# Two MLPs behind a sigmoid attention: transposes ahead of the copies, weight splits off GpSimd, output products opened early

## The chip, the cores and the metric

The kernel runs on one core of one Trainium2 chip. The time is the device time of one execution in microseconds, as the median of a few runs. The profile is of one execution; its engines are called PE (TensorE, with PEld for its weight loads), DVE (VectorE), ACT (ScalarE), POOL (GpSimd) and SP (which issues most DMAs).

## The reference

All tensors arrive as 32-bit floats, the weights of the MLPs as 64-bit floats.

```python
def attn(q, k, v):                      # 4 batches, 12 heads, 448 positions, 64 per head
    scores = 1 / sqrt(64) * q @ k.T - log(448)
    return 1 / (1 + exp(-scores)) @ v
def reference(q, k, v, ...):
    x = attn(q, k, v)                   # as 1792 tokens x 768
    h = x @ w_in1                       # 768 -> 2048
    x = (h - tanh(h)) @ w_out1          # 2048 -> 768
    h = x @ w_in2
    return (s * relu(h) ** 2 + b) @ w_out2
```

## The kernel before

The tokens are cut into two halves of 896 (two batches each). For each half the kernel runs attention for 12 pairs of heads, then layer 1, then layer 2. The instructions of each engine keep the order of the program text (`InOrder`), so the order in which the code is written is the order in which an engine takes its work, and an instruction that waits holds up all behind it on its engine.

**Attention.** `prep(i)` transposes q and k of pair i on PE into one PSUM tile of two banks (`tqk`), four transposes for q and four for k; ACT copies the q half to `qt`, DVE the k half to `kt`. `qk` makes the scores (`sc`) and the sigmoid (`af`, ACT), `av` the product with v (`o`), which ACT and DVE split into a high and a low part (`x`). Pair i+1 is prepared between the two halves of pair i's scores.

**Precision.** A product of two 32-bit values is made of three matmuls (`mm3`): high x high, high x low and low x high. The high part is a rounding copy by ACT, the low part a subtraction on DVE or POOL.

**Weights.** They come in chunks of 128 x 768. A group is four `in` chunks (f = 0 to 3), then two `out` chunks for each half `hd` of the output; there are four groups in a layer and eight group passes in a half of the tokens. Three steps run ahead of use: `w_load` (five chunks ahead), `w_conv` (three ahead, only in the first half of the tokens: ACT `wy` and three DVE instructions that write `wa`, `wa` and `wf` make a 32-bit float out of a 64-bit one, which is also kept in DRAM for the second half), and `w_split` (two ahead: ACT writes `whi`, DVE or POOL `wlo`). POOL has the `wlo` of the `out` chunks in the first half of the tokens. `w_ahead(n)` runs these steps; it is called from `hidden` (part "a" after the first block of tokens, part "b" after the second, as `fill` between the instructions of `activate`; for f = 3 only after all) and after some output products.

**Layers.** `hidden` makes one f: 18 matmuls on 512 tokens, 18 on 384 (`h`), and `activate` turns each block into `g`. In layer 1 an output product `y` is one d of three in a half: two PSUM banks, four f, two blocks of three matmuls. In layer 2 an output product `z` is one tile of 128 tokens, twelve matmuls of 384 columns. `bank` hands out five PSUM banks in turn for `h`, `y` and `z`. The outcome is copied by ACT in group 0 and added by DVE in the others; in the last group of layer 1 it is also split into `x2`, the input of layer 2.

Of the kernel before, what the change touches and what calls it, by code (L numbers as in the profile page):

```python
# [9 lines left out]
F32 = mybir.dt.float32  # L10
# [3 lines left out]
ALU = mybir.AluOpType  # L14
# [5 lines left out]
def tile_kernel(ctx, tc, q, k, v, w_in1, w_out1, w_in2, w_out2, s_in, b_in, out):  # L20
# [140 lines left out]

    done = {w_load: 0, w_conv: 0, w_split: 0}
# [60 lines left out]
    def prep(i):  # L223

        if i >= B * NP:
            return
        b = i // NP
        rq, rk, rr = (raws[i][nm] for nm in "qkr")
        both = banks("tqk")

        def transposed(ps, r, first):
# [12 lines left out]
        ready[i] = qt, kt  # L244
        avs[i] = []

# [47 lines left out]

    pos = [0]

    def hidden(layer, x, last, order=None):

        p = pos[0]
        pos[0] += 1  # L300
        w = w_t.pop(p)
        gt = g_p.tile([P, 2, T2], F32R, tag="g", name="g", bufs=4)
        ps, left = {}, [CC, CC]
        for step in order or ((0, range(CC)), (1, range(CC))):
            if callable(step):
                step()
                continue
            i, ccs = step
            n = BLOCKS[i].stop - BLOCKS[i].start
# [12 lines left out]

# [6 lines left out]
    def layer1(sb, order):  # L329

        x = [x_t[sb, cc] for cc in range(CC)]
        y_t, x2 = {}, []
        for grp in range(FC // FG):
            g = [hidden(0, x, f == FG - 1, order if grp == 0 and f == 0 else None) for f in range(FG)]
            for hd in range(2):
                ws = out_pair()
                for d in range(3):
                    dm = hd * 3 + d
                    ps = [bank("y")[:, :ns.stop - ns.start] for ns in BLOCKS]
                    for f in range(FG):  # L340
                        for i, ns in enumerate(BLOCKS):
                            o = f % 2 * HM + d * P
                            mm3(ps[i], ws[f // 2], slice(o, o + P), g[f], ns, f == 0, f == FG - 1)
                    if grp == 0:
                        y_t[dm] = x_p.tile([P, T2], F32, tag="y", name="y", bufs=7)
                    y = y_t[dm]
                    if grp == FC // FG - 1:
                        x2.append(x_p.tile([P, 2, T2], F32R, tag="x", name="x2", bufs=CC))
                    for i, ns in enumerate(BLOCKS):
                        if grp == 0:  # L350
                            act.copy(y[:, ns], ps[i])
                            continue
                        dve.tensor_tensor(out=y[:, ns], in0=ps[i], in1=y[:, ns], op=ALU.add)
                        if grp == FC // FG - 1:
                            split(x2[dm][:, 0, ns], x2[dm][:, 1, ns], y[:, ns])
                    if d < 2:
                        now(w_ahead(pos[0] - 2 + d))
        return x2

    def store(sb, t, z, cs):  # L360
# [9 lines left out]
    def layer2(sb, x, beside):  # L370

        z_t = {}
        for grp in range(FC // FG):
            g = [hidden(1, x, f == FG - 1) for f in range(FG)]
            for hd in range(2):
                cs = slice(hd * HM, (hd + 1) * HM)
                ws = out_pair()
                for t in range(T2 // P):
# [4 lines left out]
                    ps = bank("z")[:, :HM]  # L383
                    ts = slice(t * P, t * P + P)
                    for f in range(FG):
                        wh, wl = ws[f // 2]
                        fs = slice(f % 2 * HM, f % 2 * HM + HM)
                        pe.matmul(ps, g[f][:, 0, ts], wh[:, fs], start=f == 0, stop=False)
                        pe.matmul(ps, g[f][:, 0, ts], wl[:, fs], start=False, stop=False)
                        pe.matmul(ps, g[f][:, 1, ts], wh[:, fs], start=False, stop=f == FG - 1)  # L390
                    z = z_t[t]
                    if grp == 0:
                        act.copy(z[:, cs], ps)
                    else:
                        dve.tensor_tensor(out=z[:, cs], in0=ps, in1=z[:, cs], op=ALU.add)
# [20 lines left out]
    for sb in range(B // 2):  # L416
# [20 lines left out]
        layer2(sb, x2, {} if last else {2: lambda: prep(i1), 4: lambda: qk(i1, 0), 6: lambda: qk(i1, 1)})  # L437


# [28 lines left out]
```

## Time and profile before

| | |
|---|---|
| median of 3 runs | 1220.09 us (1220.08 to 1222.82) |
| the profiled execution: its own time, its span | 1218.4 us, 1216.6 us |
| PE busy | 1139.4 us, 94% of the span |
| PEld, DVE, ACT, POOL busy | 948.7, 561.2, 489.4, 67.4 us |
| mean granted PE clock | 0.986 of full |
| DMA | 123.62 MB, 102 GB/s |

The span runs from the first to the last instruction; the execution's own time is 1.8 us more. PE is the engine that is nearly always busy, and what is to be looked for is the 77 us in which it is not, and who ends each of these gaps. A PE row gives the start of a merged run of matmuls and, in brackets, how long PE sat idle before it and on whose work. Matmuls overlap, so a row's duration is longer than its step to the next row.

### The profile page before, as it was taken

How to read it: one execution, taken by the hardware profiler on the slowest of the kernel's cores; microseconds unless marked ns; L12 is line 12 of the kernel's file. 1: busy time of each engine (PE TensorE's matmuls, PEld its weight loads, DVE VectorE, ACT ScalarE, POOL GpSimd, SP SyncE). 2: the span in 40 equal slices, each digit the busy share in tenths (PEclk: the TensorE clock that was granted, in tenths of full speed). 3: DMA queues.
4: the chain of work that ended last, by engine and by line, in shares of the span. 5: the costliest groups of instructions: out<-in, count | busy, mean ns of one | idle time of the engine just before them, and what ended most of it. 6: DMA issues, size and time to landing. Idle time of an engine off the chain costs nothing. (4 is left out here: it accounts for less than half of the span.)

```text
span 1216.6 us, 14407 instructions
## 1 busy us (share of the span) xinstructions
PE 1139.4 (94%) x5760; PEld 948.7 (78%) x5760; DVE 561.2 (46%) x773; ACT 489.4 (40%) x734; POOL 67.4 (6%) x62
## 2 busy tenths in 40 slices
PE   7999999999989898989899999999999999999998
PEld 3445888888868897979784448888888889898988
DVE  0232757676676566665721114143434641434343
ACT  4664444242436453443525553330403352606060
POOL 0000102010110101020200000000000000000000
PEclk9999999999999898989899999999999999999999
DMA  5553454545444435444344311212121111111102
GB/s 145 138 161 92 156 174 144 166 141 167 144 137 136 155 117 156 144 135 150 105 139 104 85 34 39 65 39 65 40 66 49 55 53 53 52 53 45 60 13 91
DMA packets 111970, 123.62 MB, mean 102 GB/s; under 512 B 53024, under 2 KB 87328, under 8 KB 111904
## 3 DMA queue, kind: packets, MB, share of 16 engines
q1 hardware_dynamic: 110016, 122.25, 33.3%
q8 instruction: 45, 0.74, 0.2%
q10 hardware_dynamic: 1888, 0.46, 0.2%
q14 instruction: 21, 0.17, 0.0%
HBM read 92.01 MB, written 30.67 MB: 101 GB/s over the span
## 5 line engine op out<-in xcount | busy, mean ns | idle before, releaser
L79 PE MATMUL h<-x,whi 128*128 128x512 f32 (+1 forms) x1536 | 435.7, 364 | 4.3 <-ACT x L79 4.3
L79 PEld LDWEIGHTS h<-x,whi 128*128 128x128 f32 x1536 | 284.2, 188 | 40.1 <-ACT x L79 4.7
L79 PE MATMUL h<-x,wlo 128*128 128x512 f32 (+1 forms) x768 | 280.2, 365 | 0.0
L79 PE MATMUL z<-whi,g 128*128 128x384 f32 x896 | 238.1, 344 | 25.4 <-ACT whi L79 25.4
L79 PE MATMUL y<-g,whi 128*128 128x512 f32 (+1 forms) x768 | 219.3, 367 | 3.8 <-ACT whi L79 3.5
L79 PEld LDWEIGHTS z<-whi,g 128*128 128x128 f32 x896 | 167.7, 194 | 29.3 <-ACT whi L79 28.0
L79 ACT ACTIVATE t<-h 128x512 f32<-128x512 f32 (+1 forms) x128 | 69.7, 544 | 252.1 <-PE h L79 251.8
L79 PE MATMUL z<-wlo,g 128*128 128x384 f32 x448 | 154.4, 345 | 8.8 <-POOL wlo L79 6.5
L79 PEld LDWEIGHTS y<-g,whi 128*128 128x128 f32 x768 | 142.0, 188 | 23.1 <-ACT whi L79 6.3
L79 ACT CAST whi<-wf 128x768 fp32r<-128x768 f32 x128 | 105.3, 830 | 128.0 <-DVE wf L79 54.3
L79 PEld LDWEIGHTS h<-x,wlo 128*128 128x128 f32 x768 | 144.5, 188 | 15.2
L79 PE MATMUL y<-g,wlo 128*128 128x512 f32 (+1 forms) x384 | 141.7, 369 | 8.5 <-POOL wlo L79 7.5
L79 DVE TENSOR_TENSOR g<-t,g 128x512 fp32r<-128x512 f32 (+1 forms) x128 | 82.1, 641 | 88.8 <-ACT g L79 88.8
L79 DVE TENSOR_TENSOR wlo<-wf,whi 128x768 fp32r<-128x768 f32 x96 | 91.6, 954 | 56.1 <-ACT whi L79 56.1
L79 ACT ACTIVATE af<-sc,nlogs 128x896 f32<-128x896 f32 x96 | 89.1, 1007 | 55.2 <-PE sc L79 44.0
L79 PEld LDWEIGHTS z<-wlo,g 128*128 128x128 f32 x448 | 87.0, 194 | 11.2 <-POOL wlo L79 8.0
L79 DVE SCALAR_TENSOR_TENSOR wf<-wy,wa 128x768 uint32<-128x768 uint32 x64 | 89.0, 1391 | 3.8
L79 DVE TENSOR_TENSOR z<-z 128x384 f32<-128x384 f32 x84 | 46.4, 557 | 92.6 <-PE z L79 92.5
L79 PEld LDWEIGHTS y<-g,wlo 128*128 128x128 f32 x384 | 72.1, 188 | 20.6 <-POOL wlo L79 9.7
L79 POOL TENSOR_TENSOR wlo<-wf,whi 128x768 fp32r<-128x768 f32 x32 | 62.0, 1938 | 442.7 <-ACT whi L79 243.3
L79 ACT CAST g<-t 128x512 fp32r<-128x512 f32 (+1 forms) x128 | 72.6, 567 | 33.5 <-DVE t L79 31.2
L79 DVE TENSOR_TENSOR t<-h,t 128x512 f32<-128x512 f32 x64 | 39.9, 623 | 93.2 <-ACT t L79 93.2
(34 smaller groups left out, 692.2 us busy)
## 6 DMA issues: line engine op xcount, KB each, us to landing
raw<-in_moe_w_in_dram SPq DMA_DIRECT2D x32, 768.0 KB, 4.9
raw<-in_moe_w_out_dram SPq DMA_DIRECT2D x32, 768.0 KB, 4.7
win<-wf SPq DMA_DIRECT2D x32, 384.0 KB, 2.6
wout<-wf SPq DMA_DIRECT2D x32, 384.0 KB, 2.7
wf<-win SPq DMA_DIRECT2D x32, 384.0 KB, 2.9
wf<-wout SPq DMA_DIRECT2D x32, 384.0 KB, 3.1
rawq<-in_q_dram SPq DMA_DIRECT2D x48, 96.0 KB, 2.7
rawv<-in_v_dram SPq DMA_DIRECT2D x24, 192.0 KB, 2.6
```

Source lines behind the costliest of these rows:

```text
L79: return lambda *a, **kw: tc.keep_in_program_order(getattr(self.engine, name)(*a, **kw))
```

## The change

Four edits. In `prep` all eight transposes come ahead of the two copies. In `w_split` the low part is always made by DVE. In `hidden` the second `out` chunk is split right after the activation of f = 2, and layer 2's first f takes five sixths of both blocks before the last sixth. In both layers the output products of the first half `hd = 0` are opened with f = 0 to 2 (two of them in layer 1, three in layer 2) before their f = 3 matmuls come.

```diff
@@ w_split
         act.copy(hi, t)
         yield
-        eng = pool if 4 <= n < len(a_pass) and chunks[n][0] == "out" else dve
-        eng.tensor_tensor(out=lo, in0=t, in1=hi.bitcast(F32), op=ALU.subtract)
+        dve.tensor_tensor(out=lo, in0=t, in1=hi.bitcast(F32), op=ALU.subtract)
@@ prep
-        act.copy(qt, transposed(both[:, 0], rq, b % 2))
-        dve.tensor_copy(kt, transposed(both[:, 1], rk, 1 - b % 2))
+        tq, tk = transpose(both[:, 0], rq, b % 2), transpose(both[:, 1], rk, 1 - b % 2)
+        act.copy(qt, tq)
+        dve.tensor_copy(kt, tk)
@@ hidden
-                fill = iter(()) if last else w_ahead(p, "a" if left[1 - i] else "b")
+                fill = iter(()) if f == FG - 1 else w_ahead(p, "a" if left[1 - i] else "b")
                 activate(layer, ps[i], gt[:, 0, BLOCKS[i]], gt[:, 1, BLOCKS[i]], fill)
-        if last:
+                if f == FG - 2 and not left[1 - i]:
+                    now(upto(w_split, p + 3))
+        if f == FG - 1:
             now(w_ahead(p))
@@ layer1
+                def products(ds, fs):
+                    for d in ds:
+                        for i, ns in enumerate(BLOCKS):
+                            if fs[0] == 0:
+                                ps[d, i] = bank("y")[:, :ns.stop - ns.start]
+                        for f in fs:
+                            for i, ns in enumerate(BLOCKS):
+                                o = f % 2 * HM + d * P
+                                mm3(ps[d, i], ws[f // 2], slice(o, o + P), g[f], ns, f == 0, f == FG - 1)
...
+                if hd == 0:
+                    products((0, 1), range(FG - 1))
+                    products((0,), [FG - 1])
+                else:
+                    products((0,), range(FG))
+                evict(0)
+                now(w_ahead(pos[0] - 2))
+                if hd == 0:
+                    products((1,), [FG - 1])
+                else:
+                    products((1,), range(FG))
+                evict(1)
+                now(w_ahead(pos[0] - 1))
+                products((2,), range(FG))
+                evict(2)
@@ layer2
-            g = [hidden(1, x, f == FG - 1) for f in range(FG)]
+            g = [hidden(1, x, f, order if grp == 0 and f == 0 else None) for f in range(FG)]
...
+                if hd == 0:
+                    for t in range(3):
+                        products(t, range(FG - 1))
                 for t in range(T2 // P):
...
+                    products(t, [FG - 1] if hd == 0 and t < 3 else range(FG))
...
-                    if t in (0, 3):
+                    if t in (1, 3):
                         now(w_ahead(pos[0] - 2 + t // 3))
@@ the caller of layer2
+        order = [(0, range(CC - 1)), (1, range(CC - 1)), (0, [CC - 1]), (1, [CC - 1])]
+        layer2(sb, x2, order, {} if last else {2: lambda: prep(i1), 4: lambda: qk(i1, 0), 6: lambda: qk(i1, 1)})
```

`evict(d)` holds the copy, add and split that stood behind a product before.

PE in attention, the transposes of the third pair of heads, before (a bracket is what the instruction waits for):

```order
L79 MATMUL tqk<-ident,rawr 128x128 [waits DMAHW3_49,DMAHW0_49,PE_49]
L79 MATMUL tqk<-ident,rawq 128x128 [waits DMAHW7_49,DMAHW6_49]
L79 MATMUL tqk<-ident,rawq 128x128 x2
L79 MATMUL tqk<-ident,rawr 128x128 [waits Activation_49]
L79 MATMUL tqk<-ident,rawk 128x128 [waits DMAHW2_49,DMAHW1_49]
L79 MATMUL tqk<-ident,rawk 128x128 x2
L79 MATMUL sc<-qt,kt 128x448 [waits PE_49]
```

The same place of the changed kernel:

```order
L79 MATMUL tqk<-ident,rawr 128x128 [waits DMAHW3_49,DMAHW0_49,PE_49]
L79 MATMUL tqk<-ident,rawq 128x128 [waits DMAHW7_49,DMAHW6_49]
L79 MATMUL tqk<-ident,rawq 128x128 x2
L79 MATMUL tqk<-ident,rawr 128x128
L79 MATMUL tqk<-ident,rawk 128x128 [waits DMAHW2_49,DMAHW1_49]
L79 MATMUL tqk<-ident,rawk 128x128 x2
L79 MATMUL sc<-qt,kt 128x448 [waits Activation_49]
```

The order of PE's rows is the same; the first transpose for k no longer waits for ACT, and the scores behind it carry the wait for an earlier ACT instruction.

ACT at the end of the first group's f = 2 and through f = 3 in layer 1, before (`t_1059` and `t_1084` are the two blocks of f = 3):

```order
L79 CAST whi<-wf 128x768
L79 CAST g<-t_1030 128x384
L79 ACTIVATE t_1059<-h 128x512
L79 CAST g<-t_1060 128x512
L79 ACTIVATE t_1084<-h 128x384
L79 CAST g<-t_1085 128x384
L79 ACTIVATE wy<-raw 128x768
L79 CAST whi<-wf 128x768
```

The same place of the changed kernel (`t_1063` and `t_1088` are the blocks of f = 3):

```order
L79 CAST whi<-wf 128x768
L79 CAST g<-t_1030 128x384
L79 CAST whi<-wf 128x768
L79 ACTIVATE t_1063<-h 128x512
L79 CAST g<-t_1064 128x512
L79 ACTIVATE t_1088<-h 128x384
L79 CAST g<-t_1089 128x384
L79 ACTIVATE wy<-raw 128x768
```

The high part of the second `out` chunk has moved from behind f = 3's activation and a conversion to ahead of both; the DVE's low part moves with it.

PE at the start of the first output products of that group, from f = 2 of the first product on, before (`g_973` is f = 2, `g_1039` f = 3; `y_1105` and `y_1106` are the banks of the first product, `y_1149` the first bank of the second):

```order
L79 MATMUL y_1105<-g_973,whi_1101 128x512 x2
L79 MATMUL y_1105<-g_973,wlo_1102 128x512
L79 MATMUL y_1106<-g_973,whi_1101 128x384 x2
L79 MATMUL y_1106<-g_973,wlo_1102 128x384
L79 MATMUL y_1105<-g_1039,whi_1101 128x512 x2
L79 MATMUL y_1105<-g_1039,wlo_1102 128x512
L79 MATMUL y_1106<-g_1039,whi_1101 128x384 x2
L79 MATMUL y_1106<-g_1039,wlo_1102 128x384
L79 MATMUL y_1149<-g_830,whi_1033 128x512 x2
```

The same place of the changed kernel (`y_1125` and `y_1126` are now the second product):

```order
L79 MATMUL y_1105<-g_973,whi_1039 128x512 x2
L79 MATMUL y_1105<-g_973,wlo_1040 128x512
L79 MATMUL y_1106<-g_973,whi_1039 128x384 x2
L79 MATMUL y_1106<-g_973,wlo_1040 128x384
L79 MATMUL y_1125<-g_830,whi_1033 128x512 x2
L79 MATMUL y_1125<-g_830,wlo_1034 128x512
L79 MATMUL y_1126<-g_830,whi_1033 128x384 x2
L79 MATMUL y_1126<-g_830,wlo_1034 128x384
```

Eighteen matmuls of the second product now stand between f = 2 and f = 3 of the first.

## Rows read from the trace of the kernel before

**Rows 1.** Groups of PE instructions: count, busy us, mean ns, idle before and releasers.

```profile
L79 PE MATMUL z<-whi,g 128*128 128x384 f32 x896 | 238.1, 344 | 25.4 <-ACT whi L79 25.4
L79 PE MATMUL y<-g,whi 128*128 128x512 f32 (+1 forms) x768 | 219.3, 367 | 3.8 <-ACT whi L79 3.5
L79 PE MATMUL z<-wlo,g 128*128 128x384 f32 x448 | 154.4, 345 | 8.8 <-POOL wlo L79 6.5 <-DVE wlo L79 2.2
L79 PE MATMUL y<-g,wlo 128*128 128x512 f32 (+1 forms) x384 | 141.7, 369 | 8.5 <-POOL wlo L79 7.5 <-DVE wlo L79 1.0
L79 PE MATMUL tqk<-ident,rawr 128*128 128x128 f32 x48 | 16.0, 332 | 22.2 <-ACT qt L79 15.9 <-DMA rawr<-in_q_dram 5.5 <-DMA rawq<-in_q_dram 0.7
```

**Rows 2.** Timeline of one pair in attention: start us, us, instruction, idle before it.

```profile
46.14 0.33 PE L79 MATMUL tqk<-ident,rawr 128*128 128x128 f32 x1
...
47.48 0.33 PE L79 MATMUL tqk<-ident,rawr 128*128 128x128 f32 x1 [0.68 <-ACT qt L79]
...
48.06 3.28 PE L79 MATMUL sc<-qt,kt 64*128 64x448 f32 x16
48.23 0.62 DVE L79 COPY kt<-tqk 128x448 f32<-128x448 f32 x1 [0.78 <-PE tqk L79]
...
49.19 3.70 ACT L79 ACTIVATE af<-sc,nlogs 128x896 f32<-128x896 f32 x4 [1.77 <-PE sc L79]
```

**Rows 3.** PE timeline, layer 1, first half, groups 1 and 2.

```profile
203.21 0.73 PE L79 MATMUL y<-g,whi 128*128 128x512 f32 x2 [0.87 <-ACT whi L79]
...
264.56 0.73 PE L79 MATMUL y<-g,whi 128*128 128x512 f32 x2 [0.87 <-ACT whi L79]
```

**Rows 4.** Chain that ended last, second half of the tokens: start us, us, what.

```profile
881.38 26.72 PE y L79 x130
908.11 29.08 PE h L79 x144
...
940.68 26.72 PE y L79 x130
...
1000.65 28.20 PE z L79 x161
...
1062.11 28.19 PE z L79 x161
```

**Rows 5.** PE timeline, layer 2, first half, groups 0 and 3.

```profile
397.18 0.69 PE L79 MATMUL z<-whi,g 128*128 128x384 f32 x1 [4.21 <-ACT whi L79]
...
598.11 0.69 PE L79 MATMUL z<-whi,g 128*128 128x384 f32 x1 [4.20 <-ACT whi L79]
```

**Rows 6.** PE's matmuls of z in one stretch: busy, PEclk, DMA share, GB/s.

```profile
399.40:404.00 4.60, 4.56 (x14) 0.50 0.60 173
```

**Rows 7.** All engines, layer 1's third group: PE, PEld, DVE, ACT, POOL, PEclk, DMA.

```profile
290.00:350.00 60.00, 56.22 (x275) 49.34 (x274) 41.84 (x54) 21.88 (x35) 8.24 (x4) 1.00 0.46 147
```

**Rows 8.** Timelines of POOL and DVE in and after that group.

```profile
326.00 2.12 POOL L79 TENSOR_TENSOR wlo<-wf,whi 128x768 fp32r<-128x768 f32 x1 [7.43 <-ACT whi L79]
...
326.49 2.44 DVE L79 SCALAR_TENSOR_TENSOR wf<-wy,wa 128x768 uint32<-128x768 uint32 x1
...
354.07 0.96 DVE L79 SCALAR_TENSOR_TENSOR wf<-wy,wa 128x768 uint32<-128x768 uint32 x1
```

**Rows 9.** Timeline where layer 2 begins in the first half.

```profile
362.85 0.68 DVE L79 TENSOR_TENSOR y<-y 128x512 f32<-128x512 f32 x1
...
364.24 1.52 PE L79 MATMUL h<-x,whi 128*128 128x512 f32 x2 [4.26 <-ACT x L79]
...
365.96 0.56 DVE L79 TENSOR_TENSOR x<-y,x 128x384 fp32r<-128x384 f32 x1 [0.58 <-ACT x L79]
...
369.96 0.39 PE L79 MATMUL h<-x,whi 128*128 128x512 f32 x1
```

**Rows 10.** Groups of DVE and POOL: the low parts of the weights.

```profile
L79 DVE TENSOR_TENSOR wlo<-wf,whi 128x768 fp32r<-128x768 f32 x96 | 91.6, 954 | 56.1 <-ACT whi L79 56.1
L79 POOL TENSOR_TENSOR wlo<-wf,whi 128x768 fp32r<-128x768 f32 x32 | 62.0, 1938 | 442.7 <-ACT whi L79 243.3 <-DVE wa L79 170.2 <-issue 20.2
```

More of the change, by code (lines that the diff above doesn't have):

```diff
@@ L229, in prep, with transpose @@
         both = banks("tqk")
-        def transposed(ps, r, first):
+        def transpose(ps, r, first):
             o = 0 if first else SM
@@ L295, in tile_kernel, with hidden @@
     pos = [0]
-    def hidden(layer, x, last, order=None):
+    def hidden(layer, x, f, order=None):
         p = pos[0]
@@ L333, in layer1, with evict @@
         for grp in range(FC // FG):
-            g = [hidden(0, x, f == FG - 1, order if grp == 0 and f == 0 else None) for f in range(FG)]
+            g = [hidden(0, x, f, order if grp == 0 and f == 0 else None) for f in range(FG)]
             for hd in range(2):
                 ws = out_pair()
-                for d in range(3):
-                    dm = hd * 3 + d
[L339 to L343, printed above, removed]
+                ps = {}
+                def products(ds, fs):
[7 more added lines that the diff above has]
+                                mm3(ps[d, i], ws[f // 2], slice(o, o + P), g[f], ns, f == 0, f == FG - 1)
+                def evict(d):
+                    dm = hd * 3 + d
                     if grp == 0:
@@ L350, in layer1 @@
                         if grp == 0:
-                            act.copy(y[:, ns], ps[i])
+                            act.copy(y[:, ns], ps[d, i])
                             continue
-                        dve.tensor_tensor(out=y[:, ns], in0=ps[i], in1=y[:, ns], op=ALU.add)
+                        dve.tensor_tensor(out=y[:, ns], in0=ps[d, i], in1=y[:, ns], op=ALU.add)
                         if grp == FC // FG - 1:
                             split(x2[dm][:, 0, ns], x2[dm][:, 1, ns], y[:, ns])
-                    if d < 2:
-                        now(w_ahead(pos[0] - 2 + d))
+                if hd == 0:
[13 more added lines that the diff above has]
+                evict(2)
         return x2
@@ L368, in store, with layer2 @@
         sp.dma_start(out=rows[:, j, cs], in_=z[:, cs])
-    def layer2(sb, x, beside):
+    def layer2(sb, x, order, beside):
         z_t = {}
         for grp in range(FC // FG):
-            g = [hidden(1, x, f == FG - 1) for f in range(FG)]
+            g = [hidden(1, x, f, order if grp == 0 and f == 0 else None) for f in range(FG)]
             for hd in range(2):
@@ L377, in layer2, with products @@
                 ws = out_pair()
+                ps = {}
+                def products(t, fs):
+                    if fs[0] == 0:
+                        ps[t] = bank("z")[:, :HM]
+                    ts = slice(t * P, t * P + P)
+                    for f in fs:
+                        wh, wl = ws[f // 2]
+                        ms = slice(f % 2 * HM, f % 2 * HM + HM)
+                        pe.matmul(ps[t], g[f][:, 0, ts], wh[:, ms], start=f == 0, stop=False)
+                        pe.matmul(ps[t], g[f][:, 0, ts], wl[:, ms], start=False, stop=False)
+                        pe.matmul(ps[t], g[f][:, 1, ts], wh[:, ms], start=False, stop=f == FG - 1)
+                if hd == 0:
+                    for t in range(3):
+                        products(t, range(FG - 1))
                 for t in range(T2 // P):
@@ L380, in layer2 @@
                         beside[t]()
+                    products(t, [FG - 1] if hd == 0 and t < 3 else range(FG))
                     if hd == 0 and grp == 0:
                         z_t[t] = x_p.tile([P, T2], F32, tag="y", name="z", bufs=7)
[L383 to L390, printed above, removed]
                     z = z_t[t]
                     if grp == 0:
-                        act.copy(z[:, cs], ps)
+                        act.copy(z[:, cs], ps[t])
                     else:
-                        dve.tensor_tensor(out=z[:, cs], in0=ps, in1=z[:, cs], op=ALU.add)
+                        dve.tensor_tensor(out=z[:, cs], in0=ps[t], in1=z[:, cs], op=ALU.add)
                     if grp == FC // FG - 1:
                         store(sb, t, z, cs)
-                    if t in (0, 3):
+                    if t in (1, 3):
                         now(w_ahead(pos[0] - 2 + t // 3))
@@ L436, in tile_kernel @@
         last = sb + 1 == B // 2
-        layer2(sb, x2, {} if last else {2: lambda: prep(i1), 4: lambda: qk(i1, 0), 6: lambda: qk(i1, 1)})
+        order = [(0, range(CC - 1)), (1, range(CC - 1)), (0, [CC - 1]), (1, [CC - 1])]
+        layer2(sb, x2, order, {} if last else {2: lambda: prep(i1), 4: lambda: qk(i1, 0), 6: lambda: qk(i1, 1)})
 _INS = ['q', 'k', 'v', 'moe_w_in', 'moe_w_out', 'moe2_w_in', 'moe2_w_out', 'moe2_s', 'moe2_b']
```

## The prediction

> **What bounds the kernel now.** I read the groups of PE first, because PE is busy for 94% of the span: whatever it does not wait for costs nothing. Its 77 us of idleness have few causes [rows 1]: the high and low parts of `out` weights (z 25.4 + 8.8, y 3.5 + 8.5 us), the transposes for k behind ACT's copy of q (15.9, and 0.7 that is the same wait under another name), 5.5 us of start-up, and one wait of 4.26 us where layer 2 begins [rows 9]. No row shows PE waiting for an activation `g` itself. Then I read the timelines around these waits, to see how much a wait costs beyond its idle time, and the chain, which gives the pace of undisturbed matmuls: 26.72/130 = 0.2055 us for one of y, 29.08 us for a group's four f, 28.20/161 = 0.175 us for one of z [rows 4].
>
> **The transposes.** From the first transpose for q to the first for k 1.34 us pass, from there to the scores, the same four instructions without a wait, 0.58 [rows 2]. So the wait costs 0.76, somewhat more than the 0.68 of idleness. There are 24 pairs: 24 x 0.76 = 18.2 us; by idle time alone 15.9 + 0.7 = 16.6. I take 18. The copies now begin 0.58 later relative to the transposes. ACT idled 1.77 us before the sigmoids [rows 2], which covers this, and qt and kt are wanted only after two more score products of some 0.8 us each. If that cover were gone the wait would come back in front of the scores, and up to 18 us with it.
>
> **Groups of layer 1.** Undisturbed a group is 29.08 + 144 x 0.2055 = 58.7 us. In the first half the same wait returns after 61.35 us [rows 3], in the second after 59.30 [rows 4]. The change splits both first `out` chunks before f = 3's activations, that is a whole f (29.08/4 = 7.3 us) before y needs them. Three groups gain 61.35 - 58.7 = 2.7 each, 8.0 together; four gain 0.6 each, 2.5.
>
> **Groups of layer 2.** Undisturbed: 29.08 + 168 x 0.175 = 58.5 us. First half: (598.11 - 397.18)/3 = 67.0 [rows 5], so 8.5 a group, 33.9 for four. Second half: 1062.11 - 1000.65 = 61.46 [rows 4], so 2.95 a group, 11.8. Of the 8.5, 4.2 is the wait for the high part and 6.5/4 = 1.6 that for POOL's low part; the rest is PE's clock, which after these waits stands at 0.50, the 1.2 GHz level, over 4.6 us with 14 matmuls [rows 6]. Half of 4.56 us is 2.3. Without the waits it should not fall. f = 3's last activation, which stood ahead of the split, is now covered by 27 matmuls of opened products, 27 x 0.175 = 4.7 us.
>
> **POOL's work on DVE.** 32 low parts at 0.954 us [rows 10] add 30.5 us to DVE, four to a group. But a DVE conversion that runs beside POOL's 2.12 us takes 2.44 us, and 0.96 alone [rows 8]. Four POOL instructions in layer 1's third group [rows 7] thus free up to 4 x 1.48 = 5.9 us for the 3.8 added. DVE's 41.8 us of that group stay at 40 to 44, against 58.7 of PE. I cost this edit at nothing where PE covers it.
>
> **The last group of layer 1 and the start of layer 2, first half.** Here DVE is the bound: every product is added and split there between conversions, the last add starts at 362.85, and PE waits until 364.24 [rows 9]. DVE's series starts when the first product is complete. That comes 18 matmuls later (3.7 us) but without the group's 2.7 of waits, so 1.0 later. Two steps on the way each lose 1.48 of slow conversion and get 0.95 of low part: 1.05 earlier. The input thus arrives when it did. But PE has then only 6 matmuls of f = 0 left instead of 21, and the last of them wait for the second block's low part, 365.96 + 0.56 = 366.5; f = 1 starts near 367.0 instead of 369.96. Gain 3. Bounds: nothing, if the series starts later still; some 7 more, the rest of the lateness, if DVE stops binding. I take 3, because the series is DVE's own work, all in these rows.
>
> **What may be late next.** The first two products of layer 1 now finish six matmuls apart, so two DVE steps bunch. The second chunk of the other half of the output is split in the second step. First product at 42 x 0.2055 = 8.6 us; two steps of at most two adds (0.68), three conversion instructions (0.96) and a low part (0.95), 5.2 each: ready by 19.0 at most. PE wants it after 86 matmuls, 17.7. So a wait of 0 to 1.3 in groups 1 and 2 of the first half, where DVE both adds and converts; I take 2 us off in all. In group 3 it falls within DVE's lateness. In layer 2 the bunch is shorter and a third product is open.
>
> Open products also hold banks: four of five before the first is evicted. Layer 1's third group has waits of 0.9 us and more on PE [rows 3], at a clock of 1.00, the 2.4 GHz level [rows 7]; so short waits alone have not lowered it here. The Trainium skill (TensorE: Matmul & The Clock Gate, A second HAM failure mode: psum-queue depth-cycling) speaks against the edit: short idle times while a kernel cycles through PSUM banks can make the clock fall and rise again. By the row nothing is lost; by that rule, at the 2.3 us above in each of eight groups of layer 1, the sum would be 18 worse.
>
> **The sum.** 18 + 8.0 + 2.5 + 33.9 + 11.8 + 3 - 2 = 75.2 us. The profiled execution took 1218.4, so 1143.2; the median of the runs lies 1.7 above it: 1144.9, forecast 1145 us.
>
> **Rivals.**
> 1. The waits go, but bunched steps bring small ones. At up to 1.3 us in the sixteen groups, some with a falling clock, 10 to 18 us come back: 1155 to 1163. For it: DVE's spacing in rows 9 and the narrow margin above. Against: half the groups have no conversions, and layer 2 has 4.7 us of cover.
> 2. Attention gains nothing, because the copies stand later and the scores wait for qt, kt or a sigmoid's bank: 1145 + 18 = 1163. For it: ACT works 3.70 us in one run on the sigmoids behind the scores. Against: its 1.77 of idleness, and the scores' new wait is for an earlier sigmoid.
> 3. The clock falls in layer 1 from short bank waits, as above: 1163. Against: rows 7.
> 4. Slower. The early split is on ACT ahead of f = 3's activations and waits for the conversion of its chunk. If that is late, f = 3 is late, and so are the products. The opened ones hide 4.7 us; to eat 75 us in sixteen groups the split would have to be 4.7 + 75/16 = 9.4 us late in each. From there on it decides; at 10 us late the time is 1145 + 16 x 5.3 = 1230. For it: ACT and DVE take their work strictly in order. Against: the conversion is issued after f = 2's first block, and eight of the sixteen groups have none.
> 5. No difference: the gaps are filled by the bound that stands next, PE itself running slower, 1219. Against it: PE keeps the pace of rows 4 wherever it does not wait.
> 6. The input of layer 2 arrives in time too: 1145 - 7 = 1138.
>
> **Chances.** Forecast, 1140 to 1152: 0.62. Rival 1: 0.18. Rival 2: 0.07. Rival 3: 0.04. Rival 4: 0.03. Rival 5: 0.02. Rival 6: 0.04. The range for eight in ten runs from 1138 to 1160, through most of rival 1 and the higher bound of the boundary; the likeliest case's own is 1140 to 1152. Under 0.3%, about 3.7 us, a measurement of this kernel cannot tell from no change. Faster by more: 0.95 (forecast, 1, 2, 3, 6); within: 0.02; slower: 0.03.
>
> **What would show it.** Right: no PE wait on qt, none on POOL, whi and wlo gone or under 1 us each; groups of 58 to 59.5 us in both halves; granted clock near 1.00 except at layer 2's start, where 4 us or more of waits for weights and input remain in the first half; DVE conversions all at 0.96. Wrong steps: scores waiting for ACT (rival 2); y waiting for wlo in the middle of a group, or for an evicted bank (rivals 1 and 3); ACT waiting for `wf` between f = 2 and f = 3 (rival 4).

## The result and the profile after

The changed kernel takes 1134.72 us (median of 4 runs, 1134.09 to 1135.11) against 1220.19 for the kernel before on the same chip: a ratio of 0.9294, 95% interval 0.9278 to 0.931, or 85.5 us less. The forecast was 1145 with a range of 1138 to 1160, so the direction was right and the time 10.3 us better than forecast, 3 us outside the range. The profiled execution took 1135.0 us with a span of 1133.2, and a mean granted clock of 0.997 of full.

The busy times of the engines, from the page of the changed kernel:

```profile
PE 1119.3 (99%) x5760; PEld 943.6 (83%) x5760; DVE 549.1 (48%) x805; ACT 489.1 (43%) x734; POOL 5.4 (0%) x30
```

PE's 77 us of idleness are down to 14, and its busy time fell by 20 us too, with the same 5760 matmuls. DVE took over 32 low parts and yet is busy 12 us less. The groups of PE instructions that answer to [rows 1] (count, busy us, mean ns, idle before and releaser):

```profile
L79 PE MATMUL z<-whi,g 128*128 128x384 f32 x896 | 229.4, 334 | 0.0
L79 PE MATMUL y<-g,whi 128*128 128x512 f32 (+1 forms) x768 | 220.4, 368 | 2.0 <-ACT whi L79 1.9
L79 PE MATMUL z<-wlo,g 128*128 128x384 f32 x448 | 149.7, 334 | 0.0
L79 PE MATMUL y<-g,wlo 128*128 128x512 f32 (+1 forms) x384 | 142.2, 370 | 1.9 <-DVE wlo L79 1.7
L79 PE MATMUL tqk<-ident,rawr 128*128 128x128 f32 x48 | 14.9, 310 | 5.3 <-DMA rawr<-in_q_dram 5.3
```

No idle time is left in layer 2; the transposes wait only for the first load, and one wait of 1.3 us for the first `kt` stands behind it. Layer 1 keeps one wait for a high part and one for a low part. The chain that ended last shows the pace and the place that is left (start us, us, what):

```profile
128.52 29.36 PE y L79 x144
157.88 29.07 PE h L79 x144
186.94 29.36 PE y L79 x144
...
303.80 8.05 PE y L79 x39
...
311.87 0.70 DVE y L79
312.60 0.63 ACT x L79
313.25 0.69 DVE x L79
...
322.53 0.48 DVE wa L79
323.11 0.97 DVE wa L79
324.10 0.96 DVE wf L79
325.06 0.88 DVE wlo L79
325.98 14.55 PE y L79 x58
340.53 29.09 PE h L79 x144
369.62 29.12 PE z L79 x168
...
884.94 12.03 PE y L79 x58
```

A group of layer 1 takes 186.94 - 128.52 = 58.42 us, its output products 29.36 for 144 matmuls, a z group 29.12 for 168. Behind the start the chain leaves PE twice before its end, in the last group of layer 1 in each half, and runs through DVE and ACT. In the first half (311.87 to 325.98) it is add, round, low part, conversion, low part of a weight; in the second (875.35 to 884.94), which has no conversions, it costs 0.34 us (29.70 from y to h against 29.36). In the first half's last group PE waits twice (PE's timeline):

```profile
323.52 0.73 PE L79 MATMUL y<-g,whi 128*128 128x512 f32 x2 [1.89 <-ACT whi L79]
325.98 0.79 PE L79 MATMUL y<-g,wlo 128*128 128x512 f32 x1 [1.73 <-DVE wlo L79]
```

These are for the split of the second chunk of the other half `hd = 1`. From the start of y at 303.80 to that of h at 340.53 pass 36.73 us instead of 29.36: 7.4 us lost, of which 3.62 are idle and 14.55 - 12.03 = 2.5 are the slower pace of the last 58 matmuls (the same 58 stand at 884.94 in the second half). Of the other 1.2, some 0.6 show only as waits of weight loads, on PEld, while PE's row before still runs: 0.49 for a low part at 319.00, and this one, for DVE's step on a y before:

```profile
319.60 0.30 PEld L79 LDWEIGHTS y<-g,whi 128*128 128x128 f32 x2 [0.41 <-DVE y L79]
```

The stretches of that group (PE, PEld, DVE, ACT, POOL busy, PEclk, DMA share, GB/s) show why:

```profile
303.00:318.00 15.00, 15.00 (x76) 13.39 (x75) 8.68 (x14) 4.50 (x7) 0.00 (x0) 1.00 0.25 79
...
322.00:324.00 2.00, 0.48 (x2) 0.30 (x2) 1.90 (x3) 1.46 (x2) 0.00 (x0) 1.00 0.47 166
324.00:326.00 2.00, 0.27 (x3) 0.02 (x1) 1.97 (x4) 0.00 (x0) 0.00 (x0) 0.68 0.05 19
326.00:329.00 3.00, 3.00 (x8) 2.61 (x9) 1.74 (x4) 1.13 (x2) 0.00 (x0) 0.50 0.97 273
329.00:332.00 3.00, 3.00 (x11) 2.70 (x10) 2.27 (x4) 0.63 (x2) 0.00 (x0) 0.58 0.33 115
332.00:335.00 3.00, 3.00 (x16) 2.60 (x15) 2.33 (x4) 2.05 (x3) 0.00 (x0) 1.00 0.00 0
```

The clock stood at full, the 2.4 GHz level, up to the first wait, falls in the second, is at 0.50, the 1.2 GHz level, from 326 to 329 and mostly to 332, and is then full again; 8 matmuls pass in three microseconds where 16 do after. DVE works 3.87 of the 4.00 us in which PE waits.

One pair in attention, PE's timeline, answering to [rows 2]:

```profile
42.39 0.33 PE L79 MATMUL tqk<-ident,rawr 128*128 128x128 f32 x1
...
42.88 0.27 PE L79 MATMUL tqk<-ident,rawr 128*128 128x128 f32 x1
...
43.41 3.28 PE L79 MATMUL sc<-qt,kt 64*128 64x448 f32 x16
...
50.80 0.65 PE L79 MATMUL sc<-qt,kt 64*128 64x448 f32 x2
```

Four transposes for q take 0.49 us and four for k 0.53: 1.02 where it was 48.06 - 46.14 = 1.92 [rows 2]. These scores start without a wait, and a pair takes 50.80 - 43.41 = 7.39 us.

**Where the time came from.** The starts of the first matmul of each kind in PE's timeline, before and after, split the 83.4 us between the two profiled executions (1218.4 and 1135.0):

| part | forecast | profiles |
|---|---|---|
| attention, 24 pairs | 18 | 20.7 |
| layer 1, first half, three groups | 8.0 | 8.8 (3 x 2.93) |
| layer 1's last group and layer 2's start, first half | 3 | 3.5 |
| layer 2, first half, four groups | 33.9 | 34.3 (9.3, 8.1, 9.0, 7.9) |
| layer 1, second half, four groups | 2.5 | 3.1 (3 x 0.86 + 0.53) |
| layer 2, second half, four groups | 11.8 | 13.0 (4 x 3.25) |
| small waits of bunched steps | -2 | 0 |
| sum | 75.2 | 83.4 |
| from the profiled execution to the median | +1.7 | -0.3 |

The first row is the stretch from the first transpose to layer 1's first matmul in each half, 100.31 us before and 90.55 now in the first half, 92.74 and 82.92 in the second, with 0.9 for the pair inside layer 2 and 0.3 of an earlier start. A row of layer 2 in the second half is 32.38 us before (1028.69 - 996.31) and 29.12 now.

### The profile page after: what moved, and what is told of

Its sections match the earlier page's. It is cut to its first block, busy times and chain, and to the rows that moved or that the text cites. A ratio compares the mean times of both kernels' runs of the same rounds, so it can differ in the third digit from the quotient of the medians.

```text
span 1133.2 us, 14385 instructions
## 1 busy us (share of the span) xinstructions
PE 1119.3 (99%) x5760; PEld 943.6 (83%) x5760; DVE 549.1 (48%) x805; ACT 489.1 (43%) x734; POOL 5.4 (0%) x30
## 4 chain that ended last, share of the span: by engine, by line
PE 97%; DVE 2%; ACT 1%; DMA 0%; SPq 0%; issue 0%; DVEq 0%
PE h L79 41%; PE z L79 21%; PE y L79 19%; PE sc L79 7%; PE o L79 7%; PE tqk L79 2%; ACT x L79 0%; DVE y L79 0%; DVE x L79 0%; DVE wlo L79 0%; DVE wa L79 0%; DMA rawr<-in_q_dram 0%; DVE wf L79 0%; SPq L79 0%; ACT whi L79 0%
## 5 line engine op out<-in xcount | busy, mean ns | idle before, releaser
L79 PE MATMUL z<-whi,g 128*128 128x384 f32 x896 | 229.4, 334 | 0.0
L79 PEld LDWEIGHTS z<-whi,g 128*128 128x128 f32 x896 | 162.0, 188 | 1.3 <-issue 1.3
L79 PE MATMUL z<-wlo,g 128*128 128x384 f32 x448 | 149.7, 334 | 0.0
L79 DVE TENSOR_TENSOR wlo<-wf,whi 128x768 fp32r<-128x768 f32 x128 | 122.0, 953 | 52.9 <-ACT whi L79 52.9
L79 PEld LDWEIGHTS z<-wlo,g 128*128 128x128 f32 x448 | 84.1, 188 | 0.0
L79 PE MATMUL sc<-qt,kt 64*128 64x448 f32 x384 | 81.3, 561 | 1.3 <-DVE kt L79 1.3
L79 PE MATMUL o<-af,rawv 128*64 128x448 f32 x384 | 77.5, 545 | 0.0
```

What stands on the lines that cost most here:

```text
L79: return lambda *a, **kw: tc.keep_in_program_order(getattr(self.engine, name)(*a, **kw))
```

## The experiments

Ten kernels were run. The theory (A) was: each wait of the kernel before cost its idle time and something beyond it, the early split took all of the groups' waits away, and DVE in the last group of layer 1's first half is what is left. Every time is a median; the changed kernel is 1134.72.

**1. The transposes back between the copies**, in the changed kernel:

```diff
-        tq, tk = transpose(both[:, 0], rq, b % 2), transpose(both[:, 1], rk, 1 - b % 2)
-        act.copy(qt, tq)
-        dve.tensor_copy(kt, tk)
+        act.copy(qt, transpose(both[:, 0], rq, b % 2))
+        dve.tensor_copy(kt, transpose(both[:, 1], rk, 1 - b % 2))
```

> The changed kernel with the transposes for k behind ACT's copy again, nothing else. Theory A (a wait costs its idle time and a slower start of the matmuls behind it): pairs of attention every 8.29 us instead of 7.39, 24 x 0.90 = 21.5 us more, 1156 us. Theory B (my forecast's price, 0.76 a pair): 18 more, 1153. Theory C (idle time alone, 0.69 a pair): 16.6 more, 1151.

Measured: 1155.73 us (1155.64 to 1157.22), 21.0 above the changed kernel; ratio to before 0.9477 (0.946 to 0.9494). PE's waits (us in total, times, longest):

```profile
PE tqk L79 <- ACT qt L79: 16.3, 24, 0.9
```

So 24 waits with 16.3 us of idleness cost 21.0. The 4.7 on top are 0.2 a wait. The granted clock stays at 1.00 there. The row of three transposes for q lasts 0.49 us with a wait behind it or without; but without one the next transpose starts while the last still runs, 0.49 us after the first of q, and with one 1.34 - 0.68 = 0.66 of the step are not idle [rows 2]. Most of the extra price is this lost overlap, 0.17; the four transposes for k take 0.05 longer. The idle time alone is ruled out as the price, and so is my 18.

**2. The low parts of `out` weights back on GpSimd**, in the changed kernel:

```diff
-        dve.tensor_tensor(out=lo, in0=t, in1=hi.bitcast(F32), op=ALU.subtract)
+        eng = pool if 4 <= n < len(a_pass) and chunks[n][0] == "out" else dve
+        eng.tensor_tensor(out=lo, in0=t, in1=hi.bitcast(F32), op=ALU.subtract)
```

> The changed kernel with the low parts of the out chunks of the first half on POOL again. Theory A (the early split is what takes the weights out of PE's way; POOL is off the path): the conversions beside POOL take 2.44 us again, but only where DVE binds, in the last group of layer 1, does it show: 0 to 5 us more, 1135 to 1140. Theory B (POOL's share and the slow conversions were what made weights late): most of the two layers' 60 us in the first half come back in part, 1150 us or more, with PE waiting for wlo.

Measured: 1138.68 us (1137.95 to 1139.55), 4.0 more; ratio 0.9334 (0.932 to 0.9348). The size is within A. By the starts in PE's timeline some 1.8 us of it are a later input of layer 2, with 0.5 gained in the group before; 1.6 stand in front of layer 2's first output products, and 0.33 in each of the three groups behind. The last ones were not expected: PE covers DVE there. Experiment 9 shows what they are. Layer 1's first three groups lose nothing (29.36 for their products).

**3. No early split**, the rest of the change kept:

```diff
-                if f == FG - 2 and not left[1 - i]:
-                    now(upto(w_split, p + 3))
```

> The changed kernel without the split of the second out chunk behind f = 2; its output products are still opened with f = 0 to 2. Theory A (the split is the cause of the waits): the waits for whi and wlo stand at the third chunk of matmuls of each group again, since the opened products also need f = 2's weights; about 9 us in each group of layer 2 of the first half, 3 in the second, 3 and 1 in layer 1: 60 us more, 1185 to 1197. Theory B (opened products cover late weights): under 15 us more, below 1150.

Measured: 1197.0 us (1195.06 to 1199.56), 62.3 more; ratio 0.9813 (0.9794 to 0.9833). PE's groups of z show where:

```profile
L79 PE MATMUL z<-whi,g 128*128 128x384 f32 x896 | 237.1, 342 | 22.2 <-ACT whi L79 22.2
L79 PE MATMUL z<-wlo,g 128*128 128x384 f32 x448 | 153.7, 343 | 9.8 <-DVE wlo L79 9.8
```

The waits for `whi` and `wlo` are back at nearly the size of [rows 1], on products that are opened. Opened products could cover an activation that is late, but they themselves want the second chunk with their third f, so without the early split they wait for it. PE's waits on `whi` and `wlo` add up to 47.1 us against 3.6 in the changed kernel; the time is 62.3 higher, so some 19 us are lost beyond these 43.5 of idleness. About half of that is not the clock. In ten of the sixteen groups the granted clock stays at 1.00, and each still loses 0.54 to 0.61 us beyond its idle time (a z stretch of the second half 32.39 - 29.12 = 3.27 for waits of 2.15 and 0.55; a y stretch of the first 32.49 - 29.36 = 3.13 for 0.86 and 1.73). At that rate sixteen groups lose 9 us; the other 10, an estimate from the difference, are the lower clock of the six groups in which it stood at 0.87 to 0.95.

**4. No opened products**, the rest of the change kept:

```diff
-                if hd == 0:
-                    products((0, 1), range(FG - 1))
-                    products((0,), [FG - 1])
-                else:
-                    products((0,), range(FG))
+                products((0,), range(FG))
...
-                if hd == 0:
-                    for t in range(3):
-                        products(t, range(FG - 1))
...
-                    products(t, [FG - 1] if hd == 0 and t < 3 else range(FG))
+                    products(t, range(FG))
```

> The changed kernel with each output product made whole before the next one, as in the kernel before; the early split stays. Theory A (with the weights ready nothing is left to cover, since f = 3's first block is activated before the ninth matmul of z ends; and DVE gets the first product of the last group of layer 1 18 matmuls, 3.7 us, earlier): the same or up to 4 us faster, 1131 to 1136. Theory B (f = 3's activation comes late and the opened products hide it): waits for g of 1 us or more in each of 16 groups, 1150 or more.

Measured: 1132.31 us (1131.7 to 1132.73), 2.4 less than the changed kernel; ratio 0.9281 (0.9267 to 0.9295). The opened products cover nothing that the early split has left. They cost a little, because DVE gets its first finished product later in the group in which it is the bound: 1.8 us at the end of layer 1 and the start of layer 2 in the first half, 0.34 in the second. Without them the loss in that group moves: y to h takes 30.90 us there (302.77 to 333.67), and the next stretch, h to z, 33.11 instead of 29.09, since layer 2's input is now late. In PE's timeline:

```profile
321.80 0.50 PE L79 MATMUL y<-g,wlo 128*128 128x512 f32 x1 [1.27 <-DVE wlo L79]
...
340.60 0.50 PE L79 MATMUL h<-x,whi 128*128 128x512 f32 x1 [0.70 <-ACT x L79]
```

**5. Layer 2's first f in the usual order**, in the changed kernel:

```diff
-        layer2(sb, x2, order, {} if last else {2: lambda: prep(i1), 4: lambda: qk(i1, 0), 6: lambda: qk(i1, 1)})
+        layer2(sb, x2, None, {} if last else {2: lambda: prep(i1), 4: lambda: qk(i1, 0), 6: lambda: qk(i1, 1)})
```

> The changed kernel, with the tile that opens the second layer computed in the usual order (all eight rows of the first block, then all eight of the second) where the changed kernel puts the first block's last two rows, whose input tiles are made last, behind the second block's first six. Theory A: the last group of the first layer now ends so early on VectorE that the first block's last input tile is written 0.7 us (high part, 344.11) to 1.4 us (low part, 344.76) around the moment at which TensorE wants it; the order hides that, so without it the time rises by 0 to 2 us, to 1134.7 to 1136.7. Rival B: the order is worth the 3 us that the boundary's term of the sum held (4.26 us of wait before): the time rises by 3 to 5 us, to 1138 to 1140.

Measured: 1136.28 us (1135.92 to 1136.42), 1.6 more; ratio 0.9316 (0.9303 to 0.9329). The new wait in PE's timeline:

```profile
344.68 0.50 PE L79 MATMUL h<-x,whi 128*128 128x512 f32 x1 [1.02 <-ACT x L79]
```

A's size: the reordered f hides 1.0 us for ACT's part of the last input tile, 0.2 for DVE's and the restart. It is not worth the 3 us that the sum put on the boundary; most of what the boundary gained has another cause (below).

**6. Conversions further ahead**, in the changed kernel: up to three chunks more, one more from group to group, so that three of the four conversions among the output products of layer 1's last group leave them:

```diff
+    def lead(n):
+        return 3 if 23 <= n < 28 else 2 if 15 <= n < 23 else 1 if 7 <= n < 15 else 0
...
-            yield from upto(w_load, n + 5)
-            yield from upto(w_conv, n + 3)
+            e = lead(n)
+            yield from upto(w_load, n + 5 + e)
+            yield from upto(w_conv, n + 3 + e)
```

> The changed kernel, with the first pass of the weights over the conversion run up to three chunks further ahead in layer 1, one more chunk from group to group, so that three of the four conversions leave the last group of layer 1's first half and are spread over the groups before it. Theory A: in that group VectorE's row (evictions, low parts, conversions) is what TensorE waits for, 7.3 us in all (y from 303.80 to h at 340.53 is 36.73 against 29.36 in other groups), 3.62 us of it as waits and the rest as matmuls at the lower clock behind them; with the conversions gone from there TensorE gets 4 to 7 us back, 1128 to 1131. Rival B: the wait there belongs to the copies' order, not to the amount of VectorE's work, or the earlier conversions make a wait of the same size elsewhere (three more chunks must find buffers): within 2 us of 1134.7.

Measured: 1127.9 us (1127.15 to 1128.41), 6.8 less than the changed kernel; ratio 0.9245 (0.9233 to 0.9258), the fastest of all here. PE's idle waits are then these two (us in total, times, longest):

```profile
PE tqk L79 <- DMA rawr<-in_q_dram: 5.7, 1, 5.7
PE sc L79 <- DVE kt L79: 1.3, 1, 1.3
```

And its chain at the place where the changed kernel lost its time:

```profile
321.75 12.06 PE y L79 x58
333.81 29.22 PE h L79 x144
```

The 58 matmuls take 12.06 instead of 14.55, y to h 29.72 instead of 36.73, and the mean granted clock is 1.0. That it was the amount of work in that group, and not the order of the copies, is shown by this: the order is unchanged. A conversion is three DVE instructions and one of ACT; that DVE's are the ones that count is read from the stretches above: from 322 to 326 DVE is busy for 3.87 us, ACT for 1.46. What is left of the loss, 0.36, is a weight load's wait of 0.51 for a low part at 321.75.

**7. Both: no opened products, conversions ahead.** The edits of 4 and 6 together.

> The changed kernel without the opened output products (each half of the output products waits for the whole of the last activation, as before) and with the conversions up to three chunks further ahead as in the other kernel. Theory A: both act on the same 7.3 us of the last group of layer 1's first half, which the conversions cause, so their gains do not add: 1127 to 1131, within 2 us of the kernel that only converts ahead. Rival B: the opened products cost something in every group (their part of the loss is elsewhere), so that the two gains add: some 2.4 us below the kernel that only converts ahead.

Measured: 1129.18 us (1128.48 to 1129.77); ratio 0.9258 (0.9245 to 0.9271). The gains do not add, as A says; the opened products are now worth 1.3 us. They still cost 0.4 in the last group of layer 1 in each half (29.36 here, 29.72 and 29.73 in experiment 6), and save 2.05 in one stretch of layer 2 (31.17 here, 29.12 there). Without them PE waits once, where layer 2's first group has only just got its conversions back:

```profile
364.38 0.44 PE L79 MATMUL z<-whi,g 128*128 128x384 f32 x1 [1.40 <-ACT g L79]
```

This is the wait for f = 3's activation that the edit is about, in one of sixteen groups.

**8. The early split alone**, in the kernel before:

```diff
                 activate(layer, ps[i], gt[:, 0, BLOCKS[i]], gt[:, 1, BLOCKS[i]], fill)
+                if (p % 8) == FG - 2 and not left[1 - i]:
+                    now(upto(w_split, p + 3))
```

> The kernel before, with one edit of the change alone: the split of the output weights' second chunk of the second half is made one tile earlier, behind the group's third tile. GpSimd keeps its low parts, the transposes stay between the copies, the products are not opened. Theory A: this is where the groups' gain of some 60 us comes from, so the time falls to 1157 to 1165. Rival B: with GpSimd's slower low parts (1.94 us against 0.95) and without opened products the early split is late itself in the first half, so that only part comes: 1175 to 1200.

Measured: 1161.51 us (1161.38 to 1163.22); ratio 0.9527 (0.9514 to 0.954), 58.7 less than before, 69% of the whole gain from two lines. PE's waits:

```profile
PE tqk L79 <- ACT qt L79: 16.3, 24, 0.9
...
PE h L79 <- ACT x L79: 4.2, 1, 4.2
PE y L79 <- POOL wlo L79: 1.5, 1, 1.5
```

The chunk is the second one of `hd = 0`, the first half of the output. All idle waits on `whi` are gone and one of 1.5 us on GpSimd's `wlo` is left. But each z stretch of layer 2's first half takes 30.19 us instead of 29.12, 4.3 in four, with next to no idle time on PE. The weight loads wait there (PEld's timeline):

```profile
442.01 0.19 PEld L79 LDWEIGHTS z<-wlo,g 128*128 128x128 f32 x1 [0.35 <-POOL wlo L79]
...
442.75 0.19 PEld L79 LDWEIGHTS z<-whi,g 128*128 128x128 f32 x1 [0.43 <-ACT g L79]
```

A third wait, 0.43 for DVE's `g`, follows at 443.47. So with the low parts on GpSimd f = 3's activation is late as well. Experiment 4, without opened products but with the low parts on DVE, has 29.12 there; experiment 2, with GpSimd and opened products, 29.45. Opened products thus hide 0.74 of the 1.07 that GpSimd's low parts cost in such a group. These 4.3, the transposes (21.0) and 2.0 where layer 2 begins, less the 0.34 of the second half, come to 27.0; the changed kernel is 26.8 faster. A's size.

**9. Conversions ahead, low parts on GpSimd.** The edits of 2 and 6 together.

> The kernel that converts three chunks further ahead (1127.9), with the low parts of the output weights of the first half put back on GpSimd. Theory A: GpSimd's low parts cost 4.0 us in the changed kernel only because they slow the conversions (0.96 to 2.44 us) in the groups in which VectorE is what TensorE waits for; with the conversions spread no group is left in which it is, so the cost falls to 0 to 1.5 us: 1127.9 to 1129.4. Rival B: the cost is that of the later low parts themselves (1.94 us where VectorE takes 0.954), in every group: 3 to 5 us again, 1131 to 1133.

Measured: 1131.73 us (1131.25 to 1132.28), 3.8 above the kernel that only converts ahead; ratio 0.9273 (0.9259 to 0.9286). B's size, so A's reason for experiment 2 was too narrow. But B's place is not right either. The timelines of the engines where layer 2's first output products begin:

```profile
357.89 2.10 POOL L79 TENSOR_TENSOR wlo<-wf,whi 128x768 fp32r<-128x768 f32 x1 [37.25 <-ACT whi L79]
...
358.33 2.48 DVE L79 SCALAR_TENSOR_TENSOR wf<-wy,wa 128x768 uint32<-128x768 uint32 x1
360.74 0.55 DVE L79 SCALAR_TENSOR_TENSOR t<-h,t 128x384 f32<-128x384 f32 x1
...
361.32 0.71 ACT L79 ACTIVATE t<-t,b_sb,s_sb 128x384 f32<-128x384 f32 x1 [3.50 <-DVE t L79]
...
362.48 0.83 ACT L79 CAST whi<-wf 128x768 fp32r<-128x768 f32 x1
...
363.44 1.81 POOL L79 TENSOR_TENSOR wlo<-wf,whi 128x768 fp32r<-128x768 f32 x1 [3.44 <-ACT whi L79]
...
363.36 0.44 PE L79 MATMUL z<-whi,g 128*128 128x384 f32 x1 [0.47 <-ACT whi L79]
365.30 0.44 PE L79 MATMUL z<-wlo,g 128*128 128x384 f32 x1 [1.50 <-POOL wlo L79]
```

The first chunk's low part on GpSimd slows a conversion to 2.48 us. DVE's step of f = 2's activation stands behind it, ACT's two steps wait for that (3.50), the second chunk's high part stands behind them, and its low part then takes GpSimd 1.81 us, where DVE takes 0.95. PE waits at the end of this row; in this execution the stretch loses 4.1 us (33.20 against 29.12), of which 1.97 are idle, and the granted clock is 0.56 from 366 to 369. In the following three groups of layer 2 the same leaves 0.33 us each, and in layer 1's last group a wait of 0.60 before a y. Layer 1's first three groups convert too and lose nothing (29.36), so it is not every group, as B has it. So the slowed conversion and the slower low part cost together, where one chunk's steps are handed on late, however idle VectorE is on the whole; no run separates the two. The Trainium skill (SBUF — State Buffer, SBUF: two separate sides) describes it as an exclusive lock on the ports that the two engines share, held for a whole instruction: the trace agrees, the 2.48 us end 0.82 after GpSimd's 2.10, about the 0.96 that the instruction takes alone.

**10. The low parts on VectorE alone**, in the kernel before:

```diff
-        eng = pool if 4 <= n < len(a_pass) and chunks[n][0] == "out" else dve
-        eng.tensor_tensor(out=lo, in0=t, in1=hi.bitcast(F32), op=ALU.subtract)
+        dve.tensor_tensor(out=lo, in0=t, in1=hi.bitcast(F32), op=ALU.subtract)
```

> The kernel before, with one edit of the change alone: the low parts of the output weights of the first half are computed on VectorE, none on GpSimd. Theory A: VectorE gains as much from conversions that are no longer slowed (2.44 to 0.96 us) as the low parts cost it (0.954 us each), and TensorE in the first half of the kernel before waits for the late split of the last weights' chunk, which this edit leaves where it is, but the low part at its end comes from a faster engine: 0 to 25 us off, the more the more of the wait of 8.5 us a group is the GpSimd step itself. Rival B: nothing changes at all, since the high part on ScalarE is late by itself: within 3 us of 1220. The kernel that leaves only the early split away (1197.0, low parts on VectorE, transposes ahead) bears on this: 21 us of its gain are the transposes', which leaves 2 us for the low parts with the opened products.

Measured: 1216.51 us (1212.54 to 1219.61) against 1220.46; ratio 0.9959 (0.9944 to 0.9975), 3 to 7 us less. PE's groups:

```profile
L79 PE MATMUL z<-whi,g 128*128 128x384 f32 x896 | 238.3, 344 | 20.4 <-ACT whi L79 20.4
L79 PE MATMUL y<-g,wlo 128*128 128x512 f32 (+1 forms) x384 | 141.7, 369 | 8.8 <-DVE wlo L79 8.8
```

The wait for `whi` in layer 2 falls from 25.4 [rows 1] to 20.4, with the conversions at 0.96 us on average instead of 1.39; the waits behind the late split stay. This edit is worth about 4 us, whether the split is late or early. It was not forecast as a gain.

## Why the prediction was wrong: the sizes of terms, and two small steps

**The mechanism of the two large edits was right.** By the runs the early split is worth 59 to 62 us (56 forecast for the groups) and the transposes 21 (18 forecast). The small edits were not valued right: the low parts on DVE, put at nothing, are worth 4; the order of layer 2's first f, put at 3, is worth 1.6; the opened products cost 2.4 as the rest stands. Of the prediction's signs, no wait on qt and none on POOL is there, the groups take 58.4 and 58.2 us in both halves but for layer 1's last ones, and all 64 conversions take 0.96. Two signs failed: waits of 1.89 for whi and 1.73 for wlo are left, and the clock fell there, in layer 1's last group, and not at layer 2's start.

**What failed is the size of terms**, each too small, which adds up to the 10.3 us:

- *"the wait costs 0.76".* Measured 0.90 a pair, 20.7 to 21.0 in all instead of 18. The step took the four transposes for k behind the wait (0.58) as what four cost undisturbed. Undisturbed they take 0.49 and 0.53. The row that I used as the measure of an undisturbed run stood just behind a wait, and the overlap that the wait takes from the transposes before it was left out. 2.7 us.
- *"Undisturbed a group is 58.7", "58.5".* Measured 58.42 and 58.19. The pace was taken from chain pieces of 130 and 161 matmuls [rows 4] that begin where PE starts again after a wait. The first matmul there holds up the next for longer (0.34 us at 881.38, 0.22 to 0.24 otherwise), and the chain ends such a piece 0.17 later than PE's timeline starts the next (908.11 against 907.94): 26.72/130 = 0.2055 against 29.36/144 = 0.2039 now, 28.20/161 = 0.175 against 29.12/168 = 0.1733. In fifteen groups 3.0 us (0.8 + 0.6 + 0.4 + 1.2).
- *"I take 2 us off in all"* for bunched steps in groups 1 and 2. Their products take 29.36, no wait at all. 2 us. The bunching did come, with its wait for the second chunk, but in the last group, where the adds are followed by splits too; there, where the step had put it at nothing ("it falls within DVE's lateness"), it is the 3.62 us shown above.
- *"the median of the runs lies 1.7 above".* It lay 0.3 below. The 1.7 was the difference between one profiled execution and a median of three. 2.0 us.
- *The start of layer 2, "Gain 3".* 3.5, but by another way than the working, so that the number fits by luck: layer 1's last products took 2.8 us longer than before (36.73 against 33.94) and the stretch from layer 2's start to its first output products 6.3 less (29.09 against 35.38). PE had been held back itself, 7.4 us in the group before, so that the input came in time. Experiment 6 shows that these 7.4 were to be had as well: DVE's row was the bound, as the step said, and its bound "some 7 more, if DVE stops binding" is what converting ahead gives (6.8).

**The range** had its lower end at the one rival with a gain, 1138, and gave every other uncertainty to the slow side. The small errors were all of one sign, more than half of their sum because the "undisturbed" figures were read from rows that stood right behind a wait.

**The step on POOL**, "I cost this edit at nothing where PE covers it", failed by 4 us outside the groups that it had in mind: PE covers DVE's busy time, but not the order in which DVE, ACT and GpSimd hand on one chunk (experiments 9 and 10). It does not show as an error of the sum, as far as can be told, because the kernel with the edit was compared with undisturbed groups.

**The cover of 27 opened products**, "4.7 us", was not needed (experiment 4): with the chunk split early nothing late stood there. Only with the conversions moved it hid 1.4 us of idle time in one group (experiment 7), and with GpSimd's low parts 0.74 in each of four (experiments 2 and 8).

**The rivals.** Of rival 1 only the last groups of layer 1 came, 7.4 us in the first half and 0.34 in the second. Rival 2 did not: the scores start without a wait after 0.53 us of transposes. For rival 3, the groups of layer 1 with opened products run at 29.36 with the clock at 1.00 (as from 303 to 318 in the stretches above); it fell only behind the two waits of 1.89 and 1.73, which are for weights. The two rows that were put against this rival do not belong together: the waits of [rows 3] lie in other groups than the stretch of [rows 7], which has waits of 0.87 and 1.52 of its own, at 1.00. The rule of the Trainium skill on cycling through PSUM banks (TensorE: Matmul & The Clock Gate, A second HAM failure mode: psum-queue depth-cycling) took nothing here; by it the sum would have been 18 worse. Rival 4 did not come: PE shows no wait on f = 3's activation in the changed kernel. Rival 5 did not come. Rival 6 came in part: layer 2's input is in time, but its 7 us were paid in the group before, until experiment 6 got them.

What stays open: how much of the 4 us of GpSimd's low parts is the slowed conversion and how much the slower low part, and what the opened products would do in the kernel before; neither was run by itself.

## What to carry to other kernels

Price a wait by the rows on both sides of it, and take the undisturbed pace from a stretch that neither starts nor ends at a wait; here idle time alone was short by 22 and 30% (16.3 against 21.0, 43.5 against 62.3). Look at the weight loads' waits too: some cost time and show next to no idle time on PE. When a chunk's last preparation stands behind the last activation, move the preparation ahead by one tile before opening products to cover it: the first was worth 59 us, the second cost 2.4 here, and paid only where the activation was late for another reason. And after a change has cleared PE, look for the one group in which another engine has all its duties at once; moving three conversions into earlier groups gave 6.8 us more, and left PE with no idle time but the start's.

## What the hardware showed that I had not expected

- A wait of 0.68 us [rows 2] costs 0.88 (21.0/24) at a clock of 1.00: eight transposes with it take 1.24 us beyond the idle time, 1.02 without a wait, most of it overlap that is lost before the gap.
- Waits of 0.35, 0.43 and 0.43 us of weight loads show next to no idle time on PE, and yet make a group of layer 2 1.07 us longer (experiment 8).
- Two waits of 1.89 and 1.73 us within 4 us were followed by some 6 us at a granted clock of 0.50 to 0.58. In the kernel before, waits of 0.87 and 1.52 (325.92 and 328.17) stood in a stretch at 1.00 [rows 7]; in experiment 3, waits of 0.87 and 1.73 left two stretches at 1.00 and a third at 0.95.
- A DVE operation on two SBUF inputs took 2.48 us beside a GpSimd one of 2.10, and 0.96 alone, and the delay went on through ACT and GpSimd to PE.
